# Two attentions in one kernel: the memory's adds and mask multiplies go from VectorE to GpSimd, and two output tiles move by a phase

## The chip, the cores and the metric

The kernel runs on one core of one Trainium2 chip. The metric is the device time of one execution in microseconds; the lower, the better. A core has TensorE (PE in the profile, its weight loads PEld), VectorE (DVE), ScalarE (ACT), GpSimd (POOL) and SyncE (SP, which here issues nearly all DMAs). Each engine runs its own instructions strictly in their order and waits at semaphores for the others.

## What is computed

Two attentions over 2048 tokens of width 640 with 32 heads of 20 stand side by side; their outputs are concatenated. Everything is bf16 outside.

```python
# A: memory-augmented attention in 4 segments of 512 tokens, heads of 20
for s in range(4):
    logits = q_s @ k_s.T * 20**-0.5 + causal_mask
    a_dot = softmax(logits) @ v_s
    pq = phi(q_s)                        # phi(t) = t + 1 if t > 0 else exp(t)
    a_mem = (pq @ M) / (pq @ z + 1e-6)   # what earlier segments left
    o_s = g * a_mem + (1 - g) * a_dot    # g = sigmoid(beta), per head
    pk = phi(k_s); M += pk.T @ v_s; z += sum(pk)
A_out = o @ wo
# B: causal attention with a sliding window of 256 tokens
p = softmax(where(0 <= i - j < 256, q @ k.T * 20**-0.5, -1e9))
B_out = (p @ v) @ wo
out = concatenate([A_out, B_out], -1)
```

## The kernel before

The tokens are cut into four chunks of 512. Chunk by chunk the kernel does B and then A, so there are eight phases: B0, A0, B1, A1, B2, A2, B3, A3. In a phase the 32 heads are eight units of four heads (class `Unit`, number `u.g`); four heads lie on the partitions at 0, 32, 64 and 96. The score blocks of the units are gathered into packs of 512 columns (class `Phase`): 20 packs in B0 and in each A phase, 24 in B1, B2 and B3, 172 in all.

**A slot** is one turn of the loop in `body`, for one pack. Slots are numbered through from 0, so A1 has slots 64 to 83, B2 84 to 107, A2 108 to 127, B3 128 to 151 and A3 152 to 171. In a slot come, in this order:

- what was put off to this slot with `self.at` (the dictionary `after`), for example `normalise` of a unit that was weighed some slots before
- `scores` of the pack: eight or four matmuls of keys and queries into three double PSUM banks `Sc` (L491), two exponentials on ScalarE (L497) into one of six buffers `pt`, and on GpSimd one to three `affine_select`s of 128x512 (L511, L517), which zero the blocks' upper triangles
- what was put off with `at_end`
- `weigh` of a unit whose last pack lies at least two slots back (`LAG`): matmuls of the weights `pt` with the values into a PSUM bank `D`, of which there are two for all that isn't scores (L546), and a copy of it to `oc` on VectorE (L562), which SP's queue sends through a DMA transpose into `ocT`
- what `last_of` holds (the second half of phi)
- dense work for the next phase and the phase's own extra work, chosen by `pick`: projections (`proj` L293, `vproj` L353), in A phases after the first the memory's reads and updates, and output tiles.

All this is written out in program order by `manual_schedule`; there is no other scheduler. `pick` compares the planned cost done so far with the share of the phase's packs that has gone by. It uses fixed costs (1.19 for a projection, 0.79 for a quarter of the values, 0.4 for a read or an update, 0.75 for half an output tile) and a list `OUT_TILES` that says how many output tiles each phase takes from the queue of finished ones; the list sums to 29, one more than the 28 tiles that there are before `tail`, which makes A3's own four. An output tile is 128 tokens: a DMA transpose into `oT`, two halves of five matmuls each (`out_half`, L630), two casts on VectorE (L633) and a store.

**The memory.** `self.remembering` is true in A1, A2 and A3. There, eight `read`s (four token tiles by two halves) multiply `phiq` with the masked memory `mz` in PSUM, and VectorE makes of each a piece of `omem`, with three instructions (L474, L476, L477). Five `upd`s (in each of B1, A1 and A2) add the chunk's own keys and values to `macc` (L442 or L444) and write `mz`, the same times a block mask (L445); both are on VectorE.

**normalise** takes the transposed unit out of `ocT`: VectorE makes the reciprocals of the four sums per token (L595), and a multiply by them writes 320 elements per partition of the chunk's output `o_tok` (`otA` or `otB` in the profile; L601). This multiply is on GpSimd while `remembering` is true and on VectorE otherwise. As a unit is normalised three to five slots after it was weighed, the last two units of B1, B2 and B3 fall into the A phase behind them, and the last three units of A1 and A2 into the B phase behind them, where `remembering` is false. In A the memory's part `omem` is then added (L611), always on VectorE and for several units at once: in A1 and A2 after the units 3 (four units, 1280 elements), 5 and 7 (two units each, 640 elements); in A3 after unit 4 (five units, 1600), and for units 5, 6 and 7 one by one. In A3, units 6 and 7 are done in `tail`, where `remembering` is false.

In the last slot `last_turn` transposes the first 384 columns of A3's output on TensorE (L665) into `pkt`, so it needs the first five units of A3 with their memory's part.

Of the kernel before, what the change touches and what calls it, by code (L numbers as in the profile page):

```python
# [8 lines left out]
ALU = mybir.AluOpType  # L9
# [8 lines left out]
G = 8  # L18
GW = 4 * DH
KT = 5  # L20
NC = 4
CH = 512
CT = CH // P
# [1 line left out]
EPS = 1e-6  # L25
SCALE = float(DH) ** -0.5
LAG = 2
OUT_TILES = (0, 0, 2, 1, 6, 1, 7, 12)
VW = 22


# [51 lines left out]
class Kern:  # L83
# [343 lines left out]
    def upd(self, c, m, st):  # L427
        nc = self.nc
        h0 = P * m // DH
        n = (P * (m + 1) - 1) // DH - h0 + 1  # L430
        W = DH + 1
        ps = self.dtile([P, 8, W], F32)
        for tt in range(CT):
            nc.tensor.matmul(ps[:, 0:n, :], lhsT=st["kt"][:, m, tt, :],
                             rhs=self.v["A"][0][:, tt, h0:h0 + n, 0:W],
                             start=(tt == 0), stop=(tt == CT - 1))
        if m == 0:
            self.mz[c] = self.wk.tile([P, KT, 8, W], BF16, name="mz", bufs=2)
        acc = self.macc[:, m, 0:n, :]
        bmb = self.bm[:, m, 0:n].unsqueeze(2).to_broadcast([P, n, W])  # L440
        if c == 0:
            nc.vector.tensor_copy(out=acc, in_=ps[:, 0:n, :])  # L442
        else:
            nc.vector.tensor_tensor(out=acc, in0=ps[:, 0:n, :], in1=acc, op=ALU.add)  # L444
        nc.vector.tensor_tensor(out=self.mz[c][:, m, 0:n, :], in0=acc, in1=bmb, op=ALU.mult)  # L445

    def read(self, c, tt, hf):
        nc = self.nc
        if tt == 0 and hf == 0:
            self.omem = self.io.tile([P, CT, D], BF16, name="omem", bufs=1)  # L450
        W = DH + 1
        ps = self.dtile([P, 16 * W], F32)
        cols = []
        for m in range(KT):
            h0 = P * m // DH
            h1 = (P * (m + 1) - 1) // DH
            prev = (P * m - 1) // DH if m else -1
            a, b = max(h0, 16 * hf), min(h1, 16 * hf + 15)
            if a > b:
                continue  # L460
            if a == prev and any(x[2] == prev for x in cols):
                cols.append((m, a, a, h0))
                a += 1
            if a <= b:
                cols.append((m, a, b, h0))
        for n, (m, a, b, h0) in enumerate(cols):
            nc.tensor.matmul(ps[:, (a - 16 * hf) * W:(b + 1 - 16 * hf) * W],
                             lhsT=self.phiq[:, m, tt * P:(tt + 1) * P],
                             rhs=self.mz[c - 1][:, m, a - h0:b + 1 - h0, :],
                             start=(n == 0), stop=(n == len(cols) - 1))  # L470
        pv = ps[:].rearrange("p (h e) -> p h e", e=W)
        hs = slice(16 * hf, 16 * hf + 16)
        rr = self.wk.tile([P, 16], F32, name="rm", bufs=2)
        nc.vector.scalar_tensor_tensor(out=rr[:], in0=pv[:, :, DH], scalar=EPS,  # L474
                                       in1=self.ge[:, hs], op0=ALU.add, op1=ALU.mult)
        nc.vector.reciprocal(out=rr[:], in_=rr[:])  # L476
        nc.vector.tensor_tensor(  # L477
            out=self.omem[:, tt, 320 * hf:320 * hf + 320].rearrange("p (h e) -> p h e", e=DH),
            in0=pv[:, :, 0:DH], in1=rr[:].unsqueeze(2).to_broadcast([P, 16, DH]), op=ALU.mult)
# [111 lines left out]
    def normalise(self, u, tp, a=0, n=CT):  # L591
        nc = self.nc
        pv = tp.rearrange("p b (j c) -> p b j c", j=4)
        rr = self.wk.tile([P, CT, 4], F32, name="rr", bufs=2)
        nc.vector.reciprocal(out=rr[:, 0:n, :], in_=pv[:, :, :, DH])  # L595
        if u.g == 0:
            self.o_tok[u.br, u.c] = self.io.tile([P, CT, D], BF16, name="ot" + u.br, bufs=2)
        o = self.o_tok[u.br, u.c][:, a:a + n, :]
        cols = slice(GW * u.g, GW * (u.g + 1))
        eng = nc.gpsimd if self.remembering else nc.vector  # L600
        eng.tensor_tensor(out=o[:, :, cols].rearrange("p b (j e) -> p b j e", j=4),  # L601
                          in0=pv[:, :, :, 0:DH],
                          in1=rr[:, 0:n, :].unsqueeze(3).to_broadcast([P, n, 4, DH]),
                          op=ALU.mult)
        if u.br == "A" and u.c > 0:
            c0 = {3: 0, 5: 4, 7: 6}.get(u.g, u.g + 1)
            if u.c == NC - 1:
                c0 = 0 if u.g == G - 4 else u.g if u.g > G - 4 else u.g + 1
            cols = slice(GW * c0, GW * (u.g + 1))
            if cols.stop > cols.start:  # L610
                nc.vector.tensor_tensor(out=o[:, :, cols], in0=o[:, :, cols],  # L611
                                        in1=self.omem[:, a:a + n, cols], op=ALU.add)
        if u.g == G - 1 and n == CT:
            self.tiles += [(u.br, u.c, tt) for tt in range(CT)]


# [103 lines left out]
    def body(self):  # L720
# [4 lines left out]
        for n, ph in enumerate(phases):  # L725
# [5 lines left out]
            self.remembering = bool(mem)  # L731
            outs = 2 * OUT_TILES[n]
            np_ = len(ph.packs)
# [159 lines left out]
```

## Time and profile before

| what | value |
| --- | --- |
| time, median of 3 runs | 377.37 us (376.49 to 377.96) |
| the profiled execution, its own time | 376.41 us |
| its span, first to last instruction | 374.7 us |
| TensorE busy | 337.9 us (90%) |
| ScalarE busy | 338.1 us (90%) |
| VectorE busy | 261.7 us (70%) |
| GpSimd busy | 262.2 us (70%) |
| TensorE's granted clock | 0.995 of full speed |
| chain that ended last | PE 45%, ACT 30%, DVE 11%, issue 6%, DMA 5%, POOL 2% |

Busy shares are means over the whole span, over stages with different limits. A line of a group or of the timeline names the source line, the engine, the operation, the tile written and the tiles read, the shapes and how often; a remark in brackets says how long the engine had been idle before, and what ended that. A line of the waits has who waited, for whom, the sum in us, how often, and the longest.

### The profile page before, as it was taken

The numbers are of one execution on the slowest core, as the hardware profiler recorded it, in microseconds if no ns is written. First come the engines' busy times: TensorE is split into PE (matmuls) and PEld (weight loads), VectorE is DVE, ScalarE is ACT, GpSimd is POOL, SyncE is SP. The second block draws the span as 40 slices with busy tenths as digits, with TensorE's granted clock in tenths as the row PEclk, the third lists the DMA queues.
The fourth block names the chain that finished last, engine by engine and source line by source line (L and its number), as shares of the span: only waits on it lengthen the run. The fifth ranks groups of instructions, "written<-read, shape, count | busy, mean of one in ns | idle before, by whom it ended". The sixth has DMA issues, their size and how long they took to land.

```text
span 374.7 us, 10400 instructions
## 1 busy us (share of the span) xinstructions
PE 337.9 (90%) x3930; PEld 159.5 (43%) x3930; DVE 261.7 (70%) x562; ACT 338.1 (90%) x386; POOL 262.2 (70%) x414
## 2 busy tenths in 40 slices
PE   8999999999898988898989999889899999989876
PEld 4443433433434344444434345334444444544444
DVE  2456767566888788866689877777567785776554
ACT  2778989999899998999899999999899999999943
POOL 9667675555786977566688889556678888766650
PEclk9999999999999999999999999999999999999989
DMA  8964457576434958566575976728644769465512
GB/s 250 311 231 118 115 162 167 120 197 155 129 98 136 175 129 161 158 111 128 83 174 131 198 125 112 155 58 154 114 86 119 140 156 114 97 133 118 131 41 73
DMA packets 112242, 52.08 MB, mean 139 GB/s; under 512 B 81856, under 2 KB 112192, under 8 KB 112192
## 3 DMA queue, kind: packets, MB, share of 16 engines
q1 hardware_dynamic: 112048, 51.33, 61.6%
q8 instruction: 31, 0.51, 0.6%
q14 instruction: 19, 0.16, 0.2%
q10 hardware_dynamic: 144, 0.08, 0.1%
HBM read 17.05 MB, written 15.07 MB: 86 GB/s over the span
## 4 chain that ended last, share of the span: by engine, by line
PE 45%; ACT 30%; DVE 11%; issue 6%; DMA 5%; POOL 2%; POOLq 0%; ACTq 0%; DVEq 0%
ACT pt L497 27%; PE D L293 14%; PE Sc L491 8%; PE D L353 5%; PE D L546 5%; PE D L630 4%; DMA ocT<-oc 3%; ACT pe L337 3%; DVE qk L296 2%; PE D L255 2%; DMA oT<-otB 2%; DVE oc L562 2%; PE Sc L674 1%; PE D L275 1%; DVE omem L477 1%
## 5 line engine op out<-in xcount | busy, mean ns | idle before, releaser
L497 ACT ACTIVATE pt<-Sc 128x1024 bf16<-128x1024 f32 (+1 forms) x344 | 321.4, 1072 | 19.9 <-PE Sc L491 18.7
L511 POOL TENSOR_SCALAR_AFFINE_SELECT pt<-pt 128x512 bf16<-128x512 bf16 x254 | 165.7, 664 | 94.3 <-ACT pt L497 93.9
L517 POOL TENSOR_SCALAR_AFFINE_SELECT pt<-pt 128x512 bf16<-128x512 bf16 x112 | 75.9, 691 | 3.4 <-ACT pt L497 3.1
L296 DVE CAST qk<-D 128x512 bf16<-128x512 f32 x70 | 48.2, 688 | 34.0 <-PE D L293 33.7
L491 PE MATMUL Sc<-qpB,kpB 20*128 20x256 bf16 (+2 forms) x704 | 47.8, 276 | 7.3 <-ACT pt L497 5.5
L562 DVE CAST oc<-D 128x512 bf16<-128x512 f32 x46 | 31.7, 690 | 16.5 <-PE D L546 16.1
L491 PE MATMUL Sc<-qpA,kpA 20*128 20x384 bf16 (+3 forms) x512 | 38.1, 301 | 2.7 <-ACT pt L497 2.3
L491 PEld LDWEIGHTS <-kpB 20*128 20x128 bf16 x704 | 15.1, 92 | 44.3 <-issue 42.9
L630 PEld LDWEIGHTS <-oT 128*128 128x128 bf16 x280 | 24.7, 98 | 20.0 <-issue 7.8
L633 DVE CAST ot<-D 128x320 bf16<-128x320 f32 x56 | 27.1, 486 | 7.5 <-PE D L630 6.5
L353 PE MATMUL D<-Bv,xTB 128*128 128x320 bf16 x160 | 25.5, 300 | 5.0 <-DVE oc L562 3.0
L630 PE MATMUL D<-Bo,oT 128*128 128x320 bf16 x160 | 26.5, 301 | 2.5 <-DMA oT<-otB 1.9
L546 PE MATMUL D<-pt,vB 128*32 128x384 bf16 (+2 forms) x720 | 26.3, 275 | 1.0 <-DVE qk L296 0.9
L293 PE MATMUL D<-xTA,Ak 128*128 128x512 bf16 x100 | 25.0, 381 | 1.8 <-DVE oc L562 1.8
L353 PE MATMUL D<-Av,xTA 128*128 128x320 bf16 x160 | 26.3, 301 | 0.3 <-DVE vA L361 0.2
L293 PE MATMUL D<-xTA,Aq 128*128 128x512 bf16 x100 | 25.0, 381 | 0.6 <-DVE phiq L577 0.3
L546 PE MATMUL D<-pt,vA 128*32 128x256 bf16 (+3 forms) x576 | 23.9, 291 | 1.5 <-DVE pkt L668 1.5
L491 PEld LDWEIGHTS <-kpA 20*128 20x128 bf16 x512 | 11.3, 92 | 30.6 <-issue 29.3
L630 PE MATMUL D<-Ao,oT 128*128 128x320 bf16 x120 | 20.2, 300 | 1.5 <-DVE rm L474 0.9
L337 ACT ACTIVATE pe<-qk 128x512 bf16<-128x512 bf16 x30 | 21.0, 704 | 0.0
L293 PE MATMUL D<-xTB,Bk 128*128 128x512 bf16 x75 | 18.7, 380 | 2.3 <-DVE omem L477 1.9
L353 PEld LDWEIGHTS <-xTB 128*128 128x128 bf16 x160 | 14.4, 97 | 14.0 <-issue 9.3
(103 smaller groups left out, 368.7 us busy)
## 6 DMA issues: line engine op xcount, KB each, us to landing
out_dram<-ot SPq DMA_DIRECT2D x31, 160.0 KB
kdA<-qk SPq DMA_DIRECT2D x20, 128.0 KB
qdA<-qk SPq DMA_DIRECT2D x20, 128.0 KB
kdB<-qk SPq DMA_DIRECT2D x17, 128.0 KB
qdB<-qk SPq DMA_DIRECT2D x17, 128.0 KB
kpB<-kdB SPq DMA_DIRECT2D x8, 160.0 KB
qpB<-qdB SPq DMA_DIRECT2D x8, 160.0 KB
kpA<-kdA SPq DMA_DIRECT2D x8, 160.0 KB
```

The lines of the kernel that those rows point to most:

```text
L293: nc.tensor.matmul(ps[:], lhsT=self.w[br + which][:, kt, m * P:(m + 1) * P], rhs=self.xT[br][:, kt, :], start=(kt == 0), stop=(kt == KT - 1))
L296: nc.vector.tensor_copy(out=t[:], in_=ps[:])
L337: nc.scalar.activation(out=e[:], in_=t[:], func=ACT.Exp)
L353: nc.tensor.matmul(ps[:, 0:320], lhsT=self.xT[br][:, kt, tt * P:(tt + 1) * P], rhs=self.w[br + "v"][:, kt, hf * 320:(hf + 1) * 320], start ...
L491: nc.tensor.matmul(ps[j // 2][:, j % 2, off * P:(off + nq) * P], lhsT=kp[rows, u.g, k0:k0 + P], rhs=self.qp[u.br][rows, u.g, q0 * P:(q0 + ...
L497: nc.scalar.activation(out=pt[:, 2 * hp:2 * hp + 2, 0:pk.used], in_=ps[hp][:, :, 0:pk.used], func=ACT.Exp, scale=SCALE)
L511: nc.gpsimd.affine_select(out=blk, in_=blk, pattern=[[0, 4], [1, P]], compare_op=ALU.is_ge, fill=0.0, base=0, channel_multiplier=-1)
L517: nc.gpsimd.affine_select(out=blk, in_=blk, pattern=[[0, 4], [-1, P]], compare_op=ALU.is_ge, fill=0.0, base=-1, channel_multiplier=1)
L546: nc.tensor.matmul(O[32 * j:32 * j + 32, q0 * P:(q0 + nq) * P], lhsT=v[:, kt % CT, v0:v0 + 32], rhs=pt[:, j, off * P:(off + nq) * P], star ...
L562: nc.vector.tensor_copy(out=oc[:], in_=O[:])
L630: nc.tensor.matmul(ps[:, 0:320], lhsT=st["oT"][:, m, :], rhs=self.w[br + "o"][:, m, hf * 320:(hf + 1) * 320], start=(m == 0), stop=(m == K ...
L633: nc.vector.tensor_copy(out=st["ot"][:, hf * 320:(hf + 1) * 320], in_=ps[:, 0:320])
```

## The change

The adds of the memory's part are made unit by unit, by the engine that multiplied the unit. Where that is GpSimd, the add is put off by a slot, and further until all eight reads of the phase are done (`self.reads`). The multiply by the reciprocals stays on GpSimd in the same phases, but in A3 from unit 5 on it is on VectorE. The mask multiply that writes `mz` goes to GpSimd in A1 and A2. `OUT_TILES` takes one output tile less in A1 and A2 and one more in B2 and B3.

```diff
-OUT_TILES = (0, 0, 2, 1, 6, 1, 7, 12)
+OUT_TILES = (0, 0, 2, 0, 7, 0, 8, 12)
...
-        nc.vector.tensor_tensor(out=self.mz[c][:, m, 0:n, :], in0=acc, in1=bmb, op=ALU.mult)
+        eng = nc.gpsimd if self.remembering else nc.vector
+        eng.tensor_tensor(out=self.mz[c][:, m, 0:n, :], in0=acc, in1=bmb, op=ALU.mult)
 
     def read(self, c, tt, hf):
         nc = self.nc
         if tt == 0 and hf == 0:
+            self.reads = 0
             self.omem = self.io.tile([P, CT, D], BF16, name="omem", bufs=1)
+        self.reads += 1
...
-        eng = nc.gpsimd if self.remembering else nc.vector
+        pool = self.remembering and (u.br == "B" or u.c < NC - 1 or u.g < 5)
+        eng = nc.gpsimd if pool else nc.vector
         eng.tensor_tensor(out=o[:, :, cols].rearrange("p b (j e) -> p b j e", j=4),
                           in0=pv[:, :, :, 0:DH],
                           in1=rr[:, 0:n, :].unsqueeze(3).to_broadcast([P, n, 4, DH]),
                           op=ALU.mult)
+
+        def add():
+            if self.reads < 2 * CT:
+                self.at(self.slot + 1, add)
+                return
+            eng.tensor_tensor(out=o[:, :, cols], in0=o[:, :, cols],
+                              in1=self.omem[:, a:a + n, cols], op=ALU.add)
+
         if u.br == "A" and u.c > 0:
-            c0 = {3: 0, 5: 4, 7: 6}.get(u.g, u.g + 1)
-            if u.c == NC - 1:
-                c0 = 0 if u.g == G - 4 else u.g if u.g > G - 4 else u.g + 1
-            cols = slice(GW * c0, GW * (u.g + 1))
-            if cols.stop > cols.start:
-                nc.vector.tensor_tensor(out=o[:, :, cols], in0=o[:, :, cols],
-                                        in1=self.omem[:, a:a + n, cols], op=ALU.add)
+            if pool:
+                self.at(self.slot + 1, add)
+            else:
+                add()
         if u.g == G - 1 and n == CT:
+            assert not pool or u.br == "B"
             self.tiles += [(u.br, u.c, tt) for tt in range(CT)]
```

As built, the order of the instructions up to the end of B1 is the same. In A1 and A2 `pick` comes to another order of reads, updates and projections: the second read of slot 65 (109) and the read of slot 69 (113) go to slot 68 (112), where half an output tile stood, and of the five updates of slots 71 and 75 to 77 (115 and 119 to 121) three are made in slots 72 to 74 (116 to 118) and one in slot 82 (126). B2 and B3 each have two more halves of output tiles, and the halves stand partly in other slots. In A3 and in the tail TensorE's order is unchanged.

## The prediction

> **What bounds the kernel now.** I read the page first: ScalarE and TensorE are each busy for 90% of the 374.7 us span, VectorE and GpSimd for 70%. So I cut the span into phases (a phase starts with its first exponential) and asked for each engine's busy time in the last five: window and its length, then PE, PEld, DVE, ACT and POOL busy with counts, TensorE's clock, DMA share, GB/s.
>
> ```profile
> 142.90:184.10 41.20, 36.62 (x441) 17.46 (x441) 29.36 (x71) 37.83 (x41) 25.65 (x41) 1.00 0.69 131
> 184.10:233.20 49.10, 45.00 (x531) 21.00 (x530) 39.43 (x79) 49.02 (x59) 42.00 (x63) 1.00 0.73 146
> 233.20:274.10 40.90, 36.38 (x442) 17.29 (x440) 29.08 (x71) 37.78 (x41) 25.61 (x41) 1.00 0.57 116
> 274.10:322.60 48.50, 45.54 (x541) 21.49 (x540) 35.24 (x71) 47.07 (x55) 41.15 (x64) 1.00 0.66 125
> 322.60:374.70 52.10, 42.53 (x509) 23.64 (x506) 31.82 (x81) 40.11 (x47) 26.90 (x43) 0.97 0.42 98
> ```
>
> The rows are A1 (fourth phase), B2, A2, B3, A3. Slots and their packs are numbered through from 0; A1 is 64 to 83, A2 108 to 127. ScalarE's exponentials are the clock: in B2 it never rests (49.02 of 49.10). It rests 3.4 us in A1, 3.1 in A2, 1.4 in B3, and longest in A3, mostly the tail. Only those rests can be won. The waits of A1 name them:
>
> ```profile
> ACT pt L497 <- PE Sc L491: 3.1, 4, 1.3
> ...
> PE D L353 <- DVE oc L562: 1.5, 1, 1.5
> DVE otA L611 <- POOL otA L601: 1.4, 1, 1.4
> ...
> PE D L467 <- DVE oc L562: 1.0, 2, 0.5
> ```
>
> ScalarE waits for TensorE four times: 0.32, 0.75 and 0.75 us in the stretch with the memory's reads (147 to 161 us), and 1.26 us at 180.50. The timeline shows where the last comes from:
>
> ```profile
> 176.29 0.73 POOL L601 TENSOR_TENSOR otA<-ocT,rr 128x320 bf16<-128x320 bf16 x1
> ...
> 177.05 0.82 DVE L611 TENSOR_TENSOR otA<-otA,omem 128x1280 bf16<-128x1280 bf16 x1 [1.43 <-POOL otA L601]
> ...
> 178.53 1.52 PE L353 MATMUL D<-Bv,xTB 128*128 128x320 bf16 x10 [1.50 <-DVE oc L562]
> ...
> 180.50 1.02 ACT L497 ACTIVATE pt<-Sc 128x1024 bf16<-128x1024 f32 x1 [1.26 <-PE Sc L491]
> ```
>
> VectorE stands 1.43 us for GpSimd's fourth multiply, then adds for 0.82. The cast that frees a PSUM bank (L562) is queued behind until 177.80, TensorE stands 1.50, and ScalarE runs dry for 1.26. A2 repeats this (1.50 at 268.51, 1.26 at 270.48).
>
> **Part 1, the adds move.** The words promise GpSimd multiplies, but those were there: 22 before, 21 after. What is new are fifteen adds of 320 elements on GpSimd, five in each of A1, A2, A3. VectorE loses two adds of 1280 elements (826 ns), four of 640 (767) and one of 1600 (1397), and its waits for GpSimd, 6.5 us in four places. It gains six adds of 320 (325 each) and one multiply. Its adds left over follow its own multiplies, so none waits for GpSimd. The cast at 177.80 then comes when its matmuls end; next in line is ScalarE itself, which in the slots before rests at most 0.1. **A1 -1.26, A2 -1.26.**
>
> **Part 2, the mask multiply `mz` moves.** Ten in all, 380 to 400 ns on VectorE. They stood beside reads and updates, where VectorE holds TensorE for half-microseconds, but the instruction before (L444, from PSUM) stays and is what frees the bank. I take nothing for it; at best it wins the 0.42 wait per phase before an update at 167.10 and 257.08, and nothing else is late there.
>
> **Part 3, an output tile leaves A1 and A2.** A tile is two halves of five matmuls, 0.79 us a half in the chain. In A1 the halves stood in slots 68 and 83, in A2 in 112 and 126. Slot 68 is in the reads' stretch, where ScalarE's rests before packs 66 to 72 add up to 2.05 us (0.32, 0.75, 0.09, 0.14, 0.75; in A2 1.78). TensorE sets the pace there, so most of a half is won, plus a little since one pair of reads is taken apart: **A1 -0.9, A2 -0.8**. The planner also moves updates from slots 75 to 77 into 72 to 74 and one to 82; ScalarE has no rest in those slots and TensorE's sum is the same, so I cost that at nothing. Cover gone: an update, about 0.3.
>
> In B2 the tile adds 1.58 us to TensorE, which had 4.1 idle, 1.21 of it a wait at 188.67 behind the VectorE adds that shrink. ScalarE has its 2.05 us a slot against TensorE's 1.9. **Zero**; with no cover 1.58. In B3 ScalarE already rests at three places (0.64, 0.44, 0.35). The first follows a VectorE stall of 0.58 that goes (-0.6); the tile adds a half each in slots 136 and 148, close to the other two rests, so I take half of its 1.58: **B3 +0.2**. The tile's DMAs (a transpose and a store of 160 KB each) go the same way on SP's queue, past transposes of `oc`; against 7 MB moved in B2 that is 4%, cost nothing, and 1.5 us if a reciprocal again waits for its `ocT`, as once in B1.
>
> **Part 4, GpSimd's queue.** Its 22 multiplies of 320 elements (L601) each took 726 to 729 ns, so an add, also of two inputs and 320 elements, is 0.73. `mz` (147 elements, f32) isn't shown on GpSimd; between 0.19 (a select of 8 elements) and 0.73 I take 0.43, by size. GpSimd gains 15 x 0.73 + 10 x 0.43 - 0.73 = 14.5 us, 262 to 277. What matters is what queues behind: the causal selects (0.61 each in a row), and behind those the weighing matmuls. ScalarE's undisturbed slot is 1.83 us (the exponentials of packs 82 and 83 end at 182.43 and 184.27). In slots 71 to 83 of A1: 21 selects 12.8, five multiplies 3.65, five adds 3.65, five `mz` 2.15, together 22.3 of 13 x 1.83 = 23.8 us. It fits, at 94%. In slot 73, `mz` and an add behind two selects overrun the slot by about 0.5 and the selects of packs 74 to 76 come up to 0.5 late. A weigh starts when its selects end (pack 73: selects to 165.52, weigh 165.57) but reads its last pack only in its last quarter or two fifths, which hides about 0.4. I take 0.2 for each of A1 and A2.
>
> In A3 the reads end late, so three adds queue behind one multiply in slot 166: 2.8 us where 0.7 was, and the two selects of pack 166 end near 353.9 instead of 352.37. TensorE would stand 1.1 us, but at 355.73 it stands 1.52 anyway for the transpose of an output tile. That hides it; take 0.1, with no cover 1.1. **GpSimd +0.5.**
>
> The Trainium skill (GPSIMD Engine Reference, Engine selection) speaks against all of this: elementwise work belongs on VectorE, two-input operations being about twice as slow on GpSimd. The trace agrees on the price: 727 ns there, 491 at its undisturbed best on VectorE, 325 for the plain add. By its factor two, an estimate, the adds would be 0.65 and `mz` 0.77, GpSimd's stretch 23.5 of 23.8 us: the same sum, with no room left.
>
> **Part 5, the tail.**
>
> ```profile
> 356.68 1.97 POOL L511 TENSOR_SCALAR_AFFINE_SELECT pt<-pt 128x512 bf16<-128x512 bf16 x2
> 356.76 1.40 DVE L611 TENSOR_TENSOR otA<-otA,omem 128x1600 bf16<-128x1600 bf16 x1 [2.25 <-POOL otA L601]
> ...
> 360.45 0.33 DVE L611 TENSOR_TENSOR otA<-otA,omem 128x320 bf16<-128x320 bf16 x1 [1.34 <-POOL otA L601]
> ...
> 361.30 1.26 PE L546 MATMUL D<-pt,vA 128*32 128x512 bf16 x16 [1.47 <-DVE pkt L668]
> ```
>
> The sixth unit's multiply goes to VectorE, so the 1.34 wait ends: multiply and add from 358.9 end near 359.8 instead of 360.78. The copies of `pkt`, and behind them the weigh at 361.30, come up to 1.1 earlier. Against it, the fifth add now stands behind two selects on GpSimd and is done near 359.0, which delays the transposes before the copies by about 0.3. **Tail -0.8.**
>
> Sum: -2.52 - 1.7 + 0.2 + 0.5 - 0.8 = -4.3. The profiled execution took 376.41 (span 374.7 and 1.7 around it), so 372.1. The median of the three runs is 0.96 above it; I name the median's: 373.0.
>
> **Rivals.**
> *GpSimd becomes the pace (slower).* In slots 71 to 83 its new work fits only while the ten added operations average under (23.8 - 16.45) / 10 = 0.74 us; I assume 0.58. For: a select has taken up to 1.38 us instead of 0.63 while VectorE reads two SBUF operands (1.97 for two, above). Against: no multiply on GpSimd was ever stretched, and the change takes those VectorE adds away. At 1.1 us each it overruns 3.7 us in A1 and again in A2, all passed to the weighs: 373.0 + 7.4 = 380.4. The Trainium skill's rule above (GPSIMD Engine Reference, Engine selection) stands on this side.
> *The tiles cost in B2 and B3 what they weigh.* For: ScalarE has no rest in B2. Against: TensorE has 4.1 idle there. 2 x 1.58 instead of 0.8: 373.0 + 2.4 = 375.4, near no change.
> *VectorE's relief reaches further.* The reads' stretches lose their half-microsecond stalls too, and all of ScalarE's rests in A1, A2 and B3 go (7.3 us), with the tail's 0.8: 377.4 - 8.1 = 369.3. Against: those stalls belong to the read's three VectorE instructions, which stay.
>
> **Chances.** Under 0.5% (1.9 us) a difference can't be told from none. Forecast 0.60 (0.02 of it within 0.5%), relief further 0.08, tiles at full price 0.18 (0.06 faster, 0.12 same), GpSimd as the pace 0.14, slower. Together faster 0.72, same 0.14, slower 0.14. The range runs from 369.5, the relief's end, to 377.5, beyond full-priced tiles plus the tail uncovered (375.4 + 1.1), and leaves most of the GpSimd case out; the forecast's own range is 371 to 375.
>
> **What would show it.** Right: no VectorE add waiting for GpSimd; no TensorE wait of 1.5 for `oc` near 177 and 267; ScalarE's rest in A1 and A2 down from 3.4 and 3.1 to about 1.2; B2 still without rest; GpSimd near 277 us busy; the tail from the last exponential to the end (12.8 us) shorter. Wrong: TensorE waiting for selects in A1, A2 or at slot 168; an add on GpSimd far over 0.73; new ScalarE rests in B2 or B3.

## The result and the profile after

The changed kernel took 375.18 us (median of ten runs, 372.08 to 378.46); the kernel before took 377.0 (ten runs) beside it. The ratio is 0.9936, 95% interval 0.9906 to 0.9965: faster by 0.64%, some 2.4 us. The profiled execution took 375.04 us (span 373.3), 1.4 us less than before. The forecast was 4.4 us less. The profiled executions of e2 and e10, further below, were slow ones for their kernels (379.9 and 377.7 us), so the lengths of their phases are a weaker witness than those of the others.

The windows view of the changed kernel, by the same phases A1, B2, A2, B3, A3 (columns as before):

```profile
142.60:181.30 38.70, 35.70 (x425) 16.84 (x429) 25.60 (x63) 37.41 (x42) 29.77 (x50) 1.00 0.79 140
181.30:235.10 53.80, 46.59 (x535) 21.85 (x540) 41.97 (x81) 49.70 (x60) 43.11 (x67) 0.97 0.70 133
235.10:274.10 39.00, 35.81 (x425) 16.88 (x428) 25.47 (x63) 37.48 (x40) 29.15 (x48) 1.00 0.64 118
274.10:321.80 47.70, 45.50 (x546) 22.20 (x550) 35.85 (x73) 46.78 (x54) 41.45 (x65) 1.00 0.68 130
321.80:373.30 51.50, 43.22 (x509) 23.48 (x506) 31.65 (x81) 40.31 (x47) 29.65 (x47) 0.97 0.43 99
```

Against before, A1 is 2.5 us shorter, A2 1.9, B3 0.8 and A3 0.6, but **B2 is 4.7 us longer**: ScalarE, which never rested there, now rests 4.1 us. More is given back in one phase than either of the A phases won.

In A1 the waits that the forecast named are gone. VectorE has no wait for GpSimd's `otA` any more, and of ScalarE's 3.1 us for scores 1.1 are left; the timeline shows the fourth unit's multiply and, a slot later, its add, both on GpSimd, while the exponentials run through:

```profile
ACT pt L500 <- PE Sc L494: 1.1, 3, 0.7
```

```profile
161.20 21.28 ACT L500 ACTIVATE pt<-Sc 128x1024 bf16<-128x1024 f32 x23
...
175.00 0.73 POOL L605 TENSOR_TENSOR otA<-ocT,rr 128x320 bf16<-128x320 bf16 x1
...
177.32 0.79 POOL L614 TENSOR_TENSOR otA<-otA,omem 128x320 bf16<-128x320 bf16 x1
```

The groups give the prices of what moved (count, then busy us and mean ns):

```profile
L614 POOL TENSOR_TENSOR otA<-otA,omem 128x320 bf16<-128x320 bf16 x15 | 12.0, 808 | 0.0
...
L614 DVE TENSOR_TENSOR otA<-otA,omem 128x320 bf16<-128x320 bf16 x8 | 4.9, 615 | 0.3
...
L446 POOL TENSOR_TENSOR mz<-macc,bmask 128x147 bf16<-128x147 f32 x8 | 3.5, 436 | 0.0
```

Where B2 lost its time is told by the waits of that phase and by the timeline of its last 20 us:

```profile
DVE rr L598 <- DMA ocT<-oc: 3.8, 2, 3.2
...
ACT pt L500 <- PE Sc L494: 3.4, 3, 2.0
...
PE D L640 <- DVE vA L361: 2.3, 1, 2.3
```

```profile
216.26 0.53 SPq L297 DMA_DIRECT2D qdA<-qk  x1
219.79 1.51 SPq L317 DMA_DIRECT2D qpA<-qdA  x4
221.39 1.20 SPq L567 DMA_TRANSPOSE ocT<-oc  x1
...
227.34 0.25 DVE L598 RECIPROCAL rr<-ocT 128x16 f32<-128x16 bf16 x1 [3.20 <-DMA ocT<-oc]
...
228.58 0.84 PE L640 MATMUL D<-Ao,oT 128*128 128x320 bf16 x5 [2.26 <-DVE vA L361]
...
229.86 1.94 ACT L500 ACTIVATE pt<-Sc 128x1024 bf16<-128x1024 f32 x2 [2.03 <-PE Sc L494]
...
232.82 1.94 ACT L500 ACTIVATE pt<-Sc 128x1024 bf16<-128x1024 f32 x2 [1.02 <-PE Sc L494]
```

Read from the top: the copy `oc` of B2's fifth unit was ready at 218.0 (its cast on VectorE ran from 217.32). Its transpose stands on SP behind the four `qpA` loads, which read what the last `qdA` store writes and so wait until that has landed, at 219.70, 3.4 us after it was issued. The transpose goes out at 221.39 and lands 6 us later. VectorE's reciprocal stands 3.2 us for it, the casts of `vA` queue behind, TensorE stands 2.3 us for a PSUM bank, and ScalarE rests 2.03, 1.02 and 0.3 us. In the kernel before, the transpose stood behind the same loads, but the store landed sooner and the loads went out 1.9 us after it:

```profile
216.69 0.44 SPq L297 DMA_DIRECT2D qdA<-qk  x1
218.59 1.95 SPq L317 DMA_DIRECT2D qpA<-qdA  x4
220.63 1.20 SPq L564 DMA_TRANSPOSE ocT<-oc  x1
```

Its reciprocal, at 226.11, waited 0.1 us. It had only just been in time.

### The profile page after: what moved, and what is told of

The parts are those of the page before. It is cut to its first block, busy times and chain, and to the rows that moved or that the text cites. A ratio compares the mean times of both kernels' runs of the same rounds, so it can differ in the third digit from the quotient of the medians.

```text
span 373.3 us, 10343 instructions
## 1 busy us (share of the span) xinstructions
PE 336.9 (90%) x3892; PEld 159.5 (43%) x3930; DVE 257.1 (69%) x552; ACT 337.9 (91%) x386; POOL 273.9 (73%) x438
## 4 chain that ended last, share of the span: by engine, by line
PE 38%; ACT 29%; DVE 12%; DMA 7%; issue 7%; POOL 4%; SPq 2%; ACTq 0%; POOLq 0%; DVEq 0%
ACT pt L500 27%; PE D L293 13%; PE Sc L494 7%; PE D L549 5%; PE D L353 5%; PE D L640 3%; DMA ocT<-oc 3%; DVE qk L296 3%; PE D L255 2%; POOL pt L514 2%; DVE oc L565 2%; ACT pe L337 2%; DMA qpB<-qdB 2%; DMA Bk<-in_B_wqkv_dram 1%; SPq L317 1%
## 5 line engine op out<-in xcount | busy, mean ns | idle before, releaser
L514 POOL TENSOR_SCALAR_AFFINE_SELECT pt<-pt 128x512 bf16<-128x512 bf16 x254 | 164.1, 658 | 81.0 <-ACT pt L500 80.6
L520 POOL TENSOR_SCALAR_AFFINE_SELECT pt<-pt 128x512 bf16<-128x512 bf16 x112 | 74.8, 681 | 4.3 <-ACT pt L500 3.9
L494 PE MATMUL Sc<-qpB,kpB 20*128 20x256 bf16 (+2 forms) x704 | 45.7, 277 | 6.1 <-ACT pt L500 4.1
L494 PE MATMUL Sc<-qpA,kpA 20*128 20x384 bf16 (+3 forms) x512 | 40.6, 301 | 3.5 <-ACT pt L500 2.9
L643 DVE CAST ot<-D 128x320 bf16<-128x320 f32 x56 | 27.3, 487 | 11.1 <-PE D L640 10.4
L494 PEld LDWEIGHTS <-kpB 20*128 20x128 bf16 x704 | 14.6, 92 | 41.8 <-issue 40.9
L494 PEld LDWEIGHTS <-kpA 20*128 20x128 bf16 x512 | 12.2, 91 | 32.9 <-issue 30.3
L359 DVE CAST vB<-D 128x320 bf16<-128x320 f32 x32 | 15.3, 487 | 6.8 <-PE D L353 6.4
```

Source lines behind the costliest of these rows:

```text
L494: nc.tensor.matmul(ps[j // 2][:, j % 2, off * P:(off + nq) * P], lhsT=kp[rows, u.g, k0:k0 + P], rhs=self.qp[u.br][rows, u.g, q0 * P:(q0 + ...
L514: nc.gpsimd.affine_select(out=blk, in_=blk, pattern=[[0, 4], [1, P]], compare_op=ALU.is_ge, fill=0.0, base=0, channel_multiplier=-1)
L520: nc.gpsimd.affine_select(out=blk, in_=blk, pattern=[[0, 4], [-1, P]], compare_op=ALU.is_ge, fill=0.0, base=-1, channel_multiplier=1)
L643: nc.vector.tensor_copy(out=st["ot"][:, hf * 320:(hf + 1) * 320], in_=ps[:, 0:320])
```

## The experiments

The phases of all runs first. "Store to load" is the time on SP's queue from the issue of B2's last `qdA` store to the first `qpA` load; "wait" is that of the fifth unit's reciprocal in B2 for its `ocT`. Ratios are to the kernel before on the same chip; the phases come from one profiled execution each.

| kernel | ratio, 95% interval | A1 | B2 | A2 | B3 | A3 | store to load | wait |
| --- | --- | --- | --- | --- | --- | --- | --- | --- |
| before | 1 | 41.2 | 49.1 | 40.9 | 48.5 | 52.1 | 1.9 | 0.1 |
| after | 0.9936 (0.9906 to 0.9965) | 38.7 | 53.8 | 39.0 | 47.7 | 51.5 | 3.5 | 3.2 |
| e0 after again | 0.9957 (0.9924 to 0.9989) | 39.0 | 52.0 | 38.9 | 47.4 | 51.3 | 4.1 | 3.2 |
| e1 tiles of before | 0.9922 (0.9883 to 0.9961) | 41.6 | 49.2 | 39.4 | 48.4 | 50.5 | 2.0 | 0.3 |
| e2 tiles alone | 0.9969 (0.9917 to 1.0021) | 41.1 | 53.4 | 40.2 | 47.2 | 52.3 | 3.8 | 3.3 |
| e3 a slot later | 0.9905 (0.9875 to 0.9936) | 39.0 | 50.7 | 39.2 | 47.7 | 50.6 | 3.4 | 1.7 |
| e4 A1's tile back | 0.9881 (0.9816 to 0.9947) | 39.4 | 49.2 | 38.8 | 47.3 | 51.4 | 1.8 | 0.4 |
| e5 `mz` on VectorE | 0.9940 (0.9893 to 0.9987) | 39.0 | 50.6 | 39.2 | 47.9 | 50.1 | 2.0 | 1.1 |
| e6 fifth unit | 0.9838 (0.9758 to 0.9917) | 39.6 | 52.4 | 39.3 | 47.7 | 49.2 | 3.6 | 3.3 |
| e7 one DMA ahead | 0.9857 (0.9793 to 0.9921) | 39.6 | 50.0 | 38.7 | 47.3 | 50.3 | no load ahead | 0 |
| e8 e7 and e6 | 0.9785 (0.9750 to 0.9819) | 39.0 | 50.0 | 38.6 | 47.3 | 49.2 | no load ahead | 0 |
| e9 e4 and e6 | 0.9854 (0.9795 to 0.9913) | 39.4 | 51.3 | 38.8 | 47.4 | 49.1 | 3.3 | 3.0 |
| e10 e8, more on GpSimd | 0.9848 (0.9774 to 0.9921) | 38.7 | 49.2 | 38.6 | 54.8 | 49.4 | no load ahead | 0 |
| e11 e9 and e7 | 0.9774 (0.9722 to 0.9827) | 39.4 | 49.2 | 39.0 | 47.7 | 49.1 | no load ahead | 0 |

**The theory**: the tile that goes to B2 costs little itself, but it changes the order on SP's queue, and one `ocT` transpose comes too late. **The rival**: the tile costs B2 its own matmuls, which have no cover.

### The two halves of the change: e0 to e3

e0 is the changed kernel again.

> The changed kernel once more, for a second profile. Its first profile lost 4.7 us in B2 (53.8 us instead of 49.1), nearly all of it near 227 us, where a VectorE reciprocal waited 3.2 us for the transpose of oc. Theory (order): the order of SP's queue decides it, so B2 is again 53 to 54 us, with a wait of 2.5 to 4 us before that reciprocal. Rival (chance): a DMA was late by chance in that execution, B2 is near 50.5 us and the wait under 1 us. Ratio to the kernel before 0.990 to 0.997 either way.

The wait and its rest came back (3.15 us, and 1.78 of rest after it), but B2 was 52.0, less than the 53 to 54 expected.

e1 undoes the move of the tiles and keeps the rest of the change:

```diff
-OUT_TILES = (0, 0, 2, 0, 7, 0, 8, 12)
+OUT_TILES = (0, 0, 2, 1, 6, 1, 7, 12)
```

> The changed adds and mask multiplies, with the OUT_TILES of before, so that the order on TensorE and on SP is that of before. Order theory: the long wait for the transpose of oc in B2 is gone, B2 is 49 to 50 us; A1 and A2 win the 1.26 us of the add's wait each and no more, 39.9 and 39.6 us; time 0.990 to 0.994. Rival (the adds and multiplies on GpSimd make B2 slower, by their effect on VectorE): B2 stays above 52 us and the time is 0.998 or more.

B2 was 49.2 us and ScalarE did not rest in it. A2 was 39.4, 1.5 below before: the adds' part. A1 came out at 41.6 in this execution, because of rests at its start (0.56, 0.32, 1.62 and 0.46 us before packs 65 to 68; the last two are in no other run). TensorE's granted clock fell to 0.68 there, from 151 to 156 us; in e4, which is the same program up to the end of A1, it was 1.00 in that stretch and A1 took 39.4. So a phase of a single execution can be off by 2 us. The 1.26 us at the fourth add is gone all the same. With 0.9922 the adds alone do as well as the whole change.

e2 is the kernel before with the new tiles alone:

```diff
-OUT_TILES = (0, 0, 2, 1, 6, 1, 7, 12)
+OUT_TILES = (0, 0, 2, 0, 7, 0, 8, 12)
```

> The kernel before with only the new OUT_TILES: adds and mask multiplies stay on VectorE. Order theory: B2 shows the long wait again and takes 53 to 54 us, A1 and A2 win about 1 us each by the tile that leaves and keep the stall behind the add; time 1.000 to 1.006, no gain. Rival (adds): B2 at most 51 us, and the time 0.993 to 0.997.

The late wait (3.25) and a B2 of 53.4 us came with the tiles, without any of the moved adds. A2 won 0.7 and A1 0.1, where about 1 each was expected, and B3 1.3; together no change that can be told.

e3 takes away the wait by a later use, at the same order on SP:

```diff
-        late = 4 if u.br == "B" else 3 if u.c == NC - 1 else 5
+        late = (5 if u.c == 2 else 4) if u.br == "B" else 3 if u.c == NC - 1 else 5
```

> The changed kernel, but in B2 a unit is normalised five slots after its weigh instead of four, so that the reciprocal reaches VectorE about 2 us later and its transpose has landed. Order theory: the wait before the reciprocal shrinks from 3.2 us to about 1, ScalarE's rests of 2.0 and 1.0 us at the end of B2 go to at most 1 together, B2 is 50.5 to 51.5 us, ratio 0.983 to 0.989. Rival (the end of B2 is short of something else, such as TensorE's own work with the added tile): B2 stays at 53 us or more, the ratio is that of the changed kernel, 0.9936.

The reciprocal, now a slot later, waited 1.7 us instead of 3.2, ScalarE rested 0.55 there, and B2 was 50.7; the ratio, 0.9905, missed the expected 0.983 to 0.989. The tile is still in B2, so its matmuls are not what made it 53.8.

### The order on SP itself: e4 and e7, with a surprise from e5 and e9

e4 puts one tile back from B2 to A1 and leaves the move from A2 to B3:

```diff
-OUT_TILES = (0, 0, 2, 0, 7, 0, 8, 12)
+OUT_TILES = (0, 0, 2, 1, 6, 0, 8, 12)
```

> The changed kernel with one of its two tile moves undone: A1 and B2 keep the output tiles that they had before (1 and 6), A2 and B3 those of the changed kernel (0 and 8). Order theory (the ninth half more in B2 puts SP's queue in an order in which one ocT transpose comes 5 us late): B2 near 49.2 us with no reciprocal waiting over 1 us for ocT, A1 near 41, A2 39.0, B3 47.7; the whole about 1 us under the kernel with all old tiles and about 2 us under the changed one, ratio near 0.987. Rival (a tile costs what it weighs, 1.6 us wherever it goes): A2's gain comes back in B3, ratio 0.992 as with all old tiles.

B2 49.2, A2 38.8, B3 47.3, ratio 0.9881: as the order theory had it, but for A1, which took 39.4 where 41 was expected.

e7 moves one single DMA: the loads are put off by a slot, and the transpose goes ahead of them. Every other engine keeps its order.

```diff
-            self.at(self.slot + 2, lambda: self.spread(br, c, which, st, *cut[m]))
+            self.at(self.slot + (3 if (br, c, which) == ("A", 2, "q") else 2), lambda: self.spread(br, c, which, st, *cut[m]))
```

> The changed kernel with one single thing moved: on SP's queue the transpose of B2's fifth unit into ocT is issued ahead of the four qpA loads (issued a slot later) instead of behind them; all other engines' orders are the same. Order theory: the transpose is issued at about 218 instead of 221.4 us and lands in time: the reciprocal's wait of 3.2 us goes, and ScalarE's rests before packs 106 to 108 (together about 3.4 us), so B2 is near 50.4 us and the ratio near 0.987. The qpA loads come up to 1.5 us later and are not needed until A2 begins. Rival (the tile's own 1.58 us of matmuls and its DMA traffic make B2 longer): B2 stays over 52 us, and another wait stands in its place.

SP's part of its timeline, and the one line of B2's waits that has ScalarE waiting:

```profile
218.51 0.53 SPq L297 DMA_DIRECT2D qdA<-qk  x1
220.18 1.20 SPq L567 DMA_TRANSPOSE ocT<-oc  x1
222.27 1.50 SPq L317 DMA_DIRECT2D qpA<-qdA  x4
```

```profile
ACT pt L500 <- POOL pt L520: 0.7, 1, 0.7
```

The transpose goes out when its `oc` is ready; the reciprocal waits for nothing; of ScalarE's 4.1 us of rest 0.7 is left, at the start of B2. The store landed late here too: its last part at 222.19, 3.7 us after its issue, just ahead of the loads. B2 is 50.0 us with the tile in it, and the ratio is 0.9857 against e0's 0.9957, with intervals that do not meet. This shows the cause: the place of one transpose behind four waiting loads was worth 2.0 to 3.8 us (against e0 and the changed kernel; up to 1.8 of the latter may be the clock, see the last section), the tile itself 0.8 to 0.9 (against 49.2 and 49.1 without it). Of the 0.8, 0.7 is that rest at the start of B2, before pack 87: all kernels with the tile in B2 have it (0.62 to 0.72) but e10, and none of the others (at most 0.09).

e5 was meant for something else, the mask multiply back on VectorE:

```diff
-        eng = nc.gpsimd if self.remembering else nc.vector
+        eng = nc.vector
         eng.tensor_tensor(out=self.mz[c][:, m, 0:n, :], in0=acc, in1=bmb, op=ALU.mult)
```

> The changed kernel with the mask multiply mz on VectorE again in A1 and A2. Theory: the move of mz was worth nothing; A1 and A2 within 0.3 us of 38.9 and 39.0 and the ratio within 0.003 of the changed kernel's 0.995. Rival 1 (GpSimd is near its pace there, ten mz of 0.44 us hold selects back): A1 and A2 each 0.3 to 0.6 us shorter. Rival 2 (mz on VectorE held the bank of an update): each 0.4 us longer.

A1 39.0 and A2 39.2 lie among those of the kernels with `mz` on GpSimd (38.7 to 39.6, and 38.6 to 39.3), and the ratio, 0.9940, can't be told from those of the changed kernel: the move of `mz` made no difference that can be seen. But its B2, with the changed kernel's order on SP, took 50.6 us: here the store landed soon and the loads went out after 2.0 us. e9 shows the opposite, a kernel with B2's order of before in which they went out after 3.3 (the two timelines of SP, e5 then e9):

```profile
217.14 0.53 SPq L297 DMA_DIRECT2D qdA<-qk  x1
219.14 1.50 SPq L317 DMA_DIRECT2D qpA<-qdA  x4
220.74 1.21 SPq L567 DMA_TRANSPOSE ocT<-oc  x1
```

```profile
218.16 0.53 SPq L297 DMA_DIRECT2D qdA<-qk  x1
221.45 1.50 SPq L317 DMA_DIRECT2D qpA<-qdA  x4
223.05 1.20 SPq L567 DMA_TRANSPOSE ocT<-oc  x1
```

e9 is e4 with the edit of e6 (below).

> The other cure for B2: A1 and B2 keep the tiles that they had before (A2 and B3 the changed kernel's), with A3's fifth unit on VectorE. Order theory: B2 49.2 us and A1 39.4, together a little below the sum of the kernel with the DMA ahead (39.6 + 50.0); the ratio 0.982 to 0.987. Rival: A1 takes back what B2 gives, ratio 0.988 or above.

Its reciprocal waited 3.0 us and B2 took 51.3, so e9's B2 was forecast wrong. The column "store to load" puts it in order: it is either about 2 us, and the wait at most 1.1, or over 3.2, and the wait about 3 (1.7 where the use is a slot later). In the new order (after, e0, e2, e3, e5, e6) it was long in five profiled executions of six, in the old order (before, e1, e4, e9) in one of four. So the order alone does not decide it.

The traces tell the two cases apart. The store moves 128 packets of 1 KB, and its landing is told in 16 parts. In all fourteen executions 15 parts were there 1.7 to 1.9 us after the issue. In five (before, e1, e4, e5, e11) the last part came with them; in the other nine it came 3.2 to 4.0 us after the issue. Near the store, each trace has one packet of 16 KB on a queue that the profile calls `q8 instruction`, which took 0.9 to 1.5 us. In the nine it began 0.7 to 1.35 us after the store's issue, before the store's last packets had started, and 7 or 8 of the 128 started only after it had ended; in the five it began at 1.39 or later, when all of them had started. By these times one sixteenth of the store stood behind another transfer. This is read from the order in time and was not tested by an edit. The store was late in eight of the nine executions with the tile in B2 and in one of the five others; why the packet comes when it does stays open. So the theory has two halves: a transpose behind the loads has no slack, and a store that lands late then makes it late.

e11 is e9 with the one DMA ahead.

> The kernel with the tile of A1 put back and the fifth unit on VectorE, and now also with the one ocT transpose of B2 ahead of the qpA loads. With the transpose behind the loads that kernel's profiled execution had the reciprocal wait 3.0 us and a ScalarE rest of 1.8, while the same order in another kernel had a wait of 0.4 only. If the loads ahead of the transpose are what makes the wait, and the tile count only makes it likelier: no such wait, B2 49.3 us, ratio 0.977 to 0.983, like the kernel with the new tiles and the transpose ahead (0.9785). Rival (the tile itself matters in B2 beyond the order on SP): this kernel is faster than that one by over 0.3%. Second rival (the wait in that execution came from elsewhere): a wait of over 2 us for ocT remains and the ratio stays near 0.985.

No wait, B2 49.2 without rest, ratio 0.9774 instead of 0.9854 (the intervals overlap). As the store landed early in this execution, it does not show by itself that the cure works; e7, e8 and e10 do, whose store landed 3.2 to 3.7 us after its issue and whose reciprocal waited for nothing. Between e8 (0.9785, tile in B2) and e11 (tile in A1) no difference in time can be told: the tile costs B2 0.8 us and saves A1 0.4.

### The tail: e6 and e8

In the changed kernel's last slots the fifth unit's add stands behind two selects on GpSimd, and the transposes for it (L675) and the last exponentials wait:

```profile
357.88 1.09 POOL L614 TENSOR_TENSOR otA<-otA,omem 128x320 bf16<-128x320 bf16 x1
...
359.03 0.73 PE L675 MATMUL D<-ident,otA 128*128 128x128 bf16 x10 [1.80 <-POOL otA L614]
...
360.25 1.94 ACT L500 ACTIVATE pt<-Sc 128x1024 bf16<-128x1024 f32 x2 [1.79 <-PE Sc L494]
```

e6 gives that unit to VectorE:

```diff
-        pool = self.remembering and (u.br == "B" or u.c < NC - 1 or u.g < 5)
+        pool = self.remembering and (u.br == "B" or u.c < NC - 1 or u.g < 4)
```

> The changed kernel, but in A3 the fifth unit's multiply and add are made by VectorE (its add no longer stands behind two selects on GpSimd). Theory: the 1.80 us that TensorE waits before the last transposes and the 1.79 us that ScalarE rests before the last pack shrink by about 1.0 us; from the last exponential to the end 0.3 to 0.8 us shorter; the whole about 0.7 us under the changed kernel. Rival (VectorE is needed there for casts of PSUM banks, so TensorE only waits for VectorE instead): no difference, the wait keeps its length under another name.

```profile
355.43 5.69 ACT L500 ACTIVATE pt<-Sc 128x1024 bf16<-128x1024 f32 x6 [0.90 <-PE Sc L494]
356.24 0.64 DVE L614 TENSOR_TENSOR otA<-otA,omem 128x320 bf16<-128x320 bf16 x1
...
358.26 0.49 PE L675 MATMUL D<-ident,otA 128*128 128x128 bf16 x6 [0.25 <-DVE ot L643]
```

The add is done at 356.9, the transposes wait 0.25 us, and the last six exponentials run without a rest. A3 is 49.1 to 49.4 us in all five kernels with this edit, and 50.1 to 51.5 in the seven that have the change without it (mean 50.8): 1.6 us, twice what was expected.

e8 has the edits of e7 and e6.

> The changed kernel with two edits that worked alone: the one ocT transpose ahead of the qpA loads in B2, and A3's fifth unit on VectorE. If they are independent: B2 near 50 us, A3 near 49.5, and the ratio 0.982 to 0.987, faster than each alone by about half a microsecond or more. Rival (both only shift the same slack): no faster than the one DMA alone, 0.986.

370.41 us (median of six runs, 369.61 to 372.54), ratio 0.9785: the two gains add up, B2 50.0 and A3 49.2. With e11 (371.07, 369.34 to 373.39) it is the fastest version, some 2.2% faster than the kernel before.

### More on GpSimd: e10

e10 is e8, and the sixth and seventh units of A1 and A2, which fall into B2 and B3, keep multiply and add on GpSimd:

```diff
-        pool = self.remembering and (u.br == "B" or u.c < NC - 1 or u.g < 4)
+        pool = self.remembering and (u.br == "B" or u.c < NC - 1 or u.g < 4) or u.br == "A" and 0 < u.c < NC - 1 and u.g < 7
```

> The kernel with the DMA ahead and the fifth unit on VectorE, and in addition the sixth and seventh units of A1 and A2, which fall into B2 and B3, keep their multiply and add on GpSimd. VectorE loses there four multiplies of 0.56 and four adds of about 0.6 us. If the backlog on VectorE at the start of B2 (slots 84 to 88, TensorE's wait of about 1.2 us for oc and ScalarE's rest of 0.7 before pack 87) comes from these, both shrink and B2 is 0.5 us shorter. Rival (GpSimd is the pace there: selects of two blocks a pack, 42 of 50 us busy already): selects late, weighs wait for them, B2 or B3 longer by up to 1.5 us.

In B2 it did what was hoped: the rest of 0.7 us is gone, 49.2 us. In B3 it went wrong in the profiled execution, in a way that neither theory had. The timeline of B3's start:

```profile
283.85 5.96 DVE L605 TENSOR_TENSOR otA<-ocT,rr 128x320 bf16<-128x320 bf16 x1
283.98 0.79 POOL L614 TENSOR_TENSOR otA<-otA,omem 128x320 bf16<-128x320 bf16 x1
...
288.24 1.22 POOL L520 TENSOR_SCALAR_AFFINE_SELECT pt<-pt 128x512 bf16<-128x512 bf16 x2
289.84 0.33 DVE L614 TENSOR_TENSOR otA<-otA,omem 128x320 bf16<-128x320 bf16 x1
...
290.82 1.49 PE L640 MATMUL D<-Bo,oT 128*128 128x320 bf16 x5 [4.53 <-DVE qk L296]
...
292.97 1.94 ACT L500 ACTIVATE pt<-Sc 128x1024 bf16<-128x1024 f32 x2 [5.63 <-PE Sc L494]
```

One multiply on VectorE took 5.96 us instead of 0.49. It began at 283.85; from then to 289.46 GpSimd worked through an add and nine selects (one of them under way) without a gap, and the multiply ended 0.35 us after that. The one weigh that waited for a select waited 0.3 us; what stood was VectorE, and behind it a cast, TensorE 4.53 us and ScalarE 5.63. The Trainium skill (SBUF — State Buffer, SBUF: two separate sides) has VectorE operations with two SBUF inputs and GpSimd share one port pair under an exclusive lock, held for the whole of an instruction, with the other engine fully blocked. The trace agrees in kind, 5.96 us instead of 0.49 beside a busy GpSimd. Read by that rule, VectorE did not get its turn between ten of GpSimd's instructions. Elsewhere it did: the six adds left to VectorE in B2 and B3 of the changed kernel each met a running select and ended 0.17 us after it. What made the difference was not tested. The executions of e10 took 370.9 to 377.7 us and the profile is of the longest; whether the stall came in others was not shown.

## Why the prediction was right or wrong

The sign, the range and the main mechanism held; the time was 2.2 us too low, and one term, B2, makes more than all of that. That the miss of 4.7 us there shows as only 2.2 in the time is partly luck: B3 came out 1.0 us and A1 0.6 better than forecast, for reasons that were not foreseen.

**The step that failed is Part 3's "zero" for B2.** It was argued from engines: TensorE had 4.1 us idle, and ScalarE needs 2.05 us a slot against 1.9. That much is nearly right: with the transpose ahead, B2 takes 50.0 us with the tile (e7, e8) and 49.2 without it (e11), so the idle time hid half of the tile's 1.58. The tile's DMAs were costed at nothing by their bytes. What SP's queue cost was not bytes but order and landing times, and the one sentence that saw it, "1.5 us if a reciprocal again waits for its `ocT`", was left as a remark, without asking which reciprocal has how much to spare; the trace of before had one in B2 that waited 0.1 us, behind loads that wait for a store, so that a store that lands 1.5 us later had to show. It was mis-sized too: the wait was 3.2 us, and B2 grew by 2.9 (e0) to 4.7 us, against the zero. New rests of ScalarE in B2 were among the signs named for being wrong, and they came.

**Part 1** (A1 and A2, -1.26 each): right in kind and too small. With the tile left in A1 (e4, e9, e11) the phase is 39.4 us, 1.8 less than before; A2 in e1 is 1.5 less. VectorE's waits for GpSimd are gone. But its left-over adds took about 635 ns, not 325, and the 0.7 us that ScalarE rests at the start of B2 hang on these units and the tile together: the rest is gone in e10, where the units leave VectorE, and in e1, e4, e9 and e11, where the tile is not in B2.

**Part 2** (`mz`, nothing): right as far as can be seen, by e5. Its price on GpSimd, 0.43 by size, was 436 ns.

**Part 3, A1 and A2** (-0.9, -0.8): right in sign, too large. Eight kernels without the tile in A1 average 39.1 us against 39.4 with it, so 0.3; A2 loses 0.5 from e1's 39.4 to the 38.9 that the kernels after it in the table average. Both phases as a whole came near the forecast because Part 1 was too small.

**Part 3, B3** (+0.2): wrong in sign. B3 got 0.8 us shorter, and it is the tiles that did it: 48.4 in e1, where only the adds moved, 47.3 in e4, which differs from e1 in A2's and B3's tiles alone. The -0.6 for a VectorE stall that goes did not come from the adds: e1 still has that first rest, 0.58. With the tile the halves stand in other slots, and the three rests of before (0.64, 0.44 and 0.35) are down to two (0.23 and 0.57); why was not tested.

**Part 4** (GpSimd): the price 0.73 of an add was 808 ns on average, 787 at the median, and its busy time 273.9 us against "near 277". A two-input add costs 2.4 times the 325 ns of VectorE alone, where the Trainium skill (GPSIMD Engine Reference, Engine selection) has about twice. In A1 and A2 GpSimd held up no exponential by more than 0.2 us. The ten added operations average 0.62 us, under the 0.74 from which the rival "GpSimd becomes the pace" would have decided. In A3 the block in slot 166 came as described, 2.28 us for three adds, and ScalarE rested 0.20 and 0.59 before packs 168 and 169, where it had rested 0.19 and 0.51 before packs 165 and 170: 0.1 more, as forecast. In the six other kernels that keep the fifth unit on GpSimd (e0, e1, e3, e4, e5, e7) it was 0.2 to 0.4 more.

**Part 5** (tail, -0.8): the span from the last exponential to the end fell from 12.8 to 11.1 us, more than forecast, but ScalarE's rest before it rose from 0.96 to 1.79 us, because of the fifth add, whose delay was costed at 0.3. Together that is -0.9: the sum was right with both of its parts mis-sized. With slot 166 A3 came to -0.6 where -0.7 was forecast; e6 shows that this one unit was worth 1.6.

**The rival on tiles at full price** gave 375.4, next to the 375.18 measured, for a reason that e7 refutes: mostly not the tile's matmuls (0.8 us of B2) but a DMA's place. A time that fits is no proof of its mechanism. The sum of **the rival on VectorE's relief** has a slip: the rests of its rows (3.4, 3.1 and 1.4) make 7.9 us, not 7.3, and its time 368.7, below the range's lower end.

## What to carry to other kernels

When work is moved between phases, write down the new order of the issuing queue, and for each transfer behind a waiting one how long its user has to spare; a transfer whose user already waits 0.1 us has no slack for a store that lands late, whatever the bytes. Put loads that wait for a store behind transposes whose data is ready. When work goes to GpSimd, look not only at whether its queue fits but at what VectorE must do with two SBUF inputs while that queue is full (here seen in one execution).

## What the runs showed of the hardware

- In one execution of e10 a VectorE multiply of 320 elements with both inputs in SBUF took 5.96 us beside GpSimd instructions that followed each other without a gap; alone it takes 0.49.
- A VectorE add of 320 elements takes 325 ns alone and about 635 where it starts beside a running GpSimd select, 0.17 us past the select's end; the eight of the changed kernel averaged 615.
- From a store's issue to the issue of the load that reads it passed either 1.8 to 2.0 us or 3.3 to 4.1, nothing between, in ten executions. In the long cases 15 of its 16 parts had landed by 1.9 us; the last stood behind a packet of 16 KB on the profile's `q8 instruction`.
- After B2's late rest the granted TensorE clock was 0.71 to 0.86 in the changed kernel and 0.79 in e2, and 1.00 in e0 and e6, which had a rest like it. The first two have the longer B2 (53.8 and 53.4 against 52.0 and 52.4), so up to 1.8 us of the 4.7 may be the clock; what sets it was not tested.
